# Split sums for 18 of 24 late attention pairs, and a new place for some attention pairs and plain rows

## The chip, the cores and the metric

The kernel runs on one core of a Trainium2 chip. The metric is the device time of one execution in microseconds (us). Engines are named as in the profile: PE is TensorE (PEld its weight loads), DVE is VectorE, ACT is ScalarE, POOL is GpSimd, SP is SyncE, which issues the DMAs here.

## The reference

Attention over 8 batches, 8 heads, 576 positions and a head width of 64, followed by a feed-forward layer with a softplus. All data are float32. Heads 0 to 3 attend to the last 32 positions (local), heads 4 to 7 to earlier positions of the same remainder modulo 32 (strided).

```python
def _attn_ref(q, k, v):
    scores = scale * np.matmul(q, k.transpose(0, 1, 3, 2))
    rel = pos[:, None] - pos[None, :]
    mask_local = (rel >= 0) & (rel < stride)            # stride = 32
    mask_strided = (rel >= 0) & (pos[None, :] % stride == pos[:, None] % stride)
    scores = np.where(masks[None, :, :, :], scores, -1000000000.0)
    attn = np.exp(scores - np.max(scores, axis=-1, keepdims=True))
    attn = attn / (np.sum(attn, axis=-1, keepdims=True) + 1e-09)
    return np.matmul(attn, v)
def _moe_ref(x, w_in, w_out):                           # x: 4608 x 512
    h = x @ w_in                                        # 512 x 2048
    g = np.maximum(h, 0.0) + np.log1p(np.exp(-np.abs(h)))
    return g @ w_out                                    # 2048 x 512
```

`x` is the attention's output with the heads side by side, one row per token.

## The kernel before

**Feed-forward layer.** The 4608 tokens are cut into 9 chunks of 512, numbered 0 to 8, and the 2048 features into 16 rows of 128. A row f of chunk c has two products: F c.f (`hidden`, L813) forms 128 features for 512 tokens in a PSUM bank `ph`, and O c.f (`output`, L882) multiplies them by `w_out` and adds to four accumulators `py0` to `py3`, one for each 128 tokens. Each product is made of float32 numbers split into a high and a low part, in three of the four combinations, so F or O is 12 matmuls of 512 columns, some 2.7 us. Between F and O lies the row's softplus: absolute value, exponential and logarithm on ACT (L825, L828, L830), the sum on DVE (`softplus`, L837), and the split of the outcome into `gh` (ACT, L298) and `gl` (DVE, L867). There are two `ph` banks, two `u` buffers and three `g` buffers.

When the last O of a chunk is done, `result` copies each accumulator into a buffer `o` (L298 on ACT or DVE) and SP stores it (L898). These `o` tiles come from the pool `io` with four buffers, which also serves the sums of weights (`ww`, `wh`) and the stored softplus rows that are read back (`u_in`, L852).

Chunks 0, 1 and 2 are computed row by row. Chunks 3 and 4, 5 and 6, and 7 and 8 form pairs, each computed by one level of Strassen (`pair_of_chunks`, `product`, L985) on sums of x (L1010, L1016, L1026) and sums of weights (L1032 to L1055), in banks a, b and c of which the first takes a `ph` bank. Rows 7 and 15 of the chunks with even numbers, 4 and 6, are plain rows outside the pairs (`plain`). Their other rows are stored as `u` in DRAM and come back later (`spilled`), when their O is done.

**Attention.** The 64 heads of 8 batches make 32 pairs of heads, n = 0 to 31, four to a batch. Pairs 0 to 7 are done before chunk 0; pairs 8 to 31, the late ones, each finish a piece of a later chunk's x and stand among the feed-forward rows. A late pair has two blocks on TensorE. S n is its scores (`head_scores`, L439): 36 matmul instructions in float32, each a pair of passes of 64 rows x 32 columns over 64 keys. V n is its weighted sums (`late_sums`). In the usual joint step S n is followed at once by V n-1; the sums' halves then go into the rest of S n's bank `po` and into a `ph` bank. A V that stands alone uses the banks `po` and `ps`.

Between S n and V n lies the softmax: mask and copy from PSUM (L498), maximum, subtraction, exponential on ACT (L513), row sums, reciprocal, multiplication (L542), and `turn`, which transposes blocks of 32x32 on DVE. After V n the pieces of x are cast into the tiles `x_h`, `x_l` and, for the chunk after next, `x_far` (`x_part`, ACT L730 and DVE L728).

A late pair has one of two forms. `WHOLE` says which, and before it holds all 24.

- Whole: part 1 of the scores uses the same column groups as part 0 (`place_of`, L421), so four tiles of the array are in use. `turn` is one transposition of 128x576 (L567). The sums (L600) take 32 key rows x 64 columns and up to 64 queries, 38 matmul instructions, 76 passes. `load_v` has four DMAs.
- Split: part 1 of the scores uses the other column groups, eight tiles. `turn` is one transposition of 128x576 (L571), which leaves half of the blocks in the wrong rows, and four of 32x288 (L576, L578), which set those right. The sums (L613) take 64 key rows x 64 columns over 32 queries, 36 matmul instructions, 72 passes. `load_v` has three DMAs and, where the pair before was whole, a memset on POOL (L335).

The scores of pairs 4 to 7 are in the split form's layout already.

**The order of the work.** Every step is a task for a `Plan` (L77): a name, an urgency, an engine, a cost in us and the tasks it comes after. The plan places the tasks by urgency into the engines' free spans and then writes them out by start time, which fixes each engine's order. The urgency of feed-forward steps follows a table of times `when`; `places` says behind which row each late pair stands; `far_first` is the last pair that stands ahead of the first chunk pair; the events in `pair_of_chunks` place the others. No scheduler moves anything after that.

Of the kernel before, what the change touches and what calls it, by code (L numbers as in the profile page):

```python
# [18 lines left out]
P = 128  # L19
# [57 lines left out]
class Plan:  # L77
# [8 lines left out]
    def add(self, name, urgency, engine, cost, fn, after=(), late=0.0):  # L86
        self.tasks[name] = (urgency, len(self.tasks), engine, cost, fn, after, late)
# [29 lines left out]
def attention_softplus_ffn(  # L117
# [9 lines left out]
    nc = tc.nc  # L127
    B, NPAIR, _, _, S = qk.shape
# [4 lines left out]
    NFC = DFF // P  # L133
# [10 lines left out]
    TPC = max(CH) // P  # L144
# [94 lines left out]
    taken = []  # L239
    phs, us, ghs, gls, lent = {}, {}, {}, {}, {}  # L240
    HALF = NFC // 2
    WHOLE = range(2 * NPAIR, 8 * NPAIR)
    NEAR = 3
    SPILLED = (NEAR + 1, NEAR + 3)
    PLAIN = [(c, f) for c in SPILLED for f in (HALF - 1, NFC - 1)]
# [961 lines left out]
    steps = [(c, f) for c in range(NEAR) for f in range(NFC)]  # L1207
# [1 line left out]
    steps += [(NEAR, HALF - 1), (NEAR, NFC - 1), (NEAR + 1, HALF - 1)]  # L1209
    begin = NFC + AHEAD  # L1210
    last = len(order) - 1
    far_first = 5 * NPAIR
    places = (0, 2, 5, 8, 11, 14, 16, 18, 20, 23, 25, 27, 30)
    pair_at = {begin + i: n for i, n in zip(places, range(2 * NPAIR, far_first + 1))}
    i_of = {n: i for i, n in pair_at.items()}
    alone = (last - NPAIR - 3, last - NPAIR, last)

    def joint(i):
        return pair_at.get(i, 0) > 2 * NPAIR
# [1 line left out]
    when = {}  # L1221
    t = 0.0
# [6 lines left out]
    add = plan.add  # L1229
# [18 lines left out]
    for i in range(begin, len(steps)):  # L1248
        c, f = steps[i]
        w, x = CH[c] / 384, when[i]  # L1250
# [15 lines left out]
        k = i - LAG  # L1266
        if k >= FAR0:
            continue
        c, f = steps[k]
        w = CH[c] / 384  # L1270
        x = when[i] + 2.1 * w
# [5 lines left out]
        for t in range(nt):  # L1277
# [4 lines left out]
            if f == NFC - 1:  # L1282
                e, cost, engine = (("ACT", 0.5, nc.scalar), ("DVE", 0.6, nc.vector))[t % 2]
# [15 lines left out]
    def sums_of(n):  # L1299
        late_sums(n, n not in alone)  # L1300
# [44 lines left out]
    def parts_of(n, z, made):  # L1345

        first = order[n][0] * S
        free = []
        for c in range(NCHUNK):
            if START[c] < first + S and START[c] + CH[c] > first:  # L1350
                old = [k for k in range(c) if PLACE[k] == PLACE[c]]
                if old and old[-1] >= NEAR:
                    free += [f"P{p}.{NEAR}.{HALF-2}" for p in "1256374"]
                elif old:
                    free.append(f"F{NFC * old[-1] + NFC - 1}")
                elif PLACE[c] == 3:
                    free.append(f"F{2 * NFC - 1}")
                    for g in range(12, NFC):
                        free += [f"Wt{g}", f"W1.{g-HALF}"]
        for half in range(2):  # L1360
            z += 0.6
            fn = lambda half=half: x_part(n, half, False)
            add(f"H{n}{half}", z, "ACT", 0.35, fn, [made] + free)
            fn = lambda half=half: x_part(n, half, True)
            add(f"L{n}{half}", z + 0.3, "DVE", 0.45, fn, [f"H{n}{half}"], 0.5)
        if n != last:
            add(f"v{n+1}", z + 2, "SP", 1.3, lambda: load_v(n + 1), [made], 2.0)

    for i, n in pair_at.items():
        x = when[i]  # L1370
        after, cost = needs_of(n), 1.3
        if joint(i):
            cost = 2.5
            after += [f"P{n-1}", f"v{n-1}", f"u{i-1}"]
        y = x + (12 if n == far_first else 1.5)
        scores_of(n, x, y, f"S{n}", "PE", cost, after, n - 1 if joint(i) else None)
        if n != far_first:
            parts_of(n, when[i_of[n + 1]] + 1.9, f"S{n+1}")

    SLOT = 0.234  # L1380
    now = when[len(steps)]
# [11 lines left out]
    def out_task(c, f, t, late=()):  # L1393

        name, own = f"O{c}.{f}.{t}", [f"l{g_of(c, f)}"]
        if c >= NEAR and f == ROWS[c][0]:
            free = f"y{FAR0 - 1 if c == NEAR else c - 1}.{t}"
            if c == NCHUNK - 1 and t == 0:
                free = f"j1.{c-1}.{HALF-1}"
            own.append(free)  # L1400
        on_pe(name, 3, lambda: output(c, f, (t,)), own)
        if f != ROWS[c][-1]:
            return
        if c == NCHUNK - 1 and t == TPC - 1:
            for h, (e, engine) in enumerate((("DVE", nc.vector), ("ACT", nc.scalar))):
                cols = slice(DM // 2 * h, DM // 2 * (h + 1))
                fn = lambda engine=engine, cols=cols: result(c, t, engine, cols)
                add(f"y{c}.{t}{h}", now, e, 0.35, fn, [name])
            return
        e, cost, engine = (("ACT", 0.6, nc.scalar), ("DVE", 0.7, nc.vector))[t % 2 * (c not in (NEAR, NEAR + 2))]  # L1410
        add(f"y{c}.{t}", now, e, cost, lambda: result(c, t, engine), [name, *late])

    g_users = [(NEAR - 1, NFC - 1), (NEAR, HALF - 1), (NEAR, NFC - 1)]
# [37 lines left out]
    def x_task(A, z, each, then=0.0):  # L1451

        for i in range(2):
            x_sums(A, i, z + (10 * each + then) * i, each)
# [214 lines left out]
    def plain(c, f):  # L1669

        on_pe(f"F{c}.{f}", 12, lambda: hidden(c, f), [ring[-2], *lows_of(c), *row_loads.get(f, [])])
        ring.append(f"u{c}.{f}")
        soft_task(c, f, f"F{c}.{f}")

    def spilled(A, rows, between, finish=None):

        C, end = A + 1, HALF - 2
        for g in ROWS[A][-2:]:
            for t in range(TPC):
                out_task(A, g, t)  # L1680
        if finish:
            finish()
        stored = {g: f"Us{g_of(C, g)}" for g in ROWS[C]}
        start = now
        for k, g in enumerate(ROWS[C]):
            z = start + 12 * SLOT * (k - 1)
            z += sum(slots * SLOT for at, slots, _ in between if at < k)
            if k < 2:
                after, z = [], z - 6
            elif k < 4:  # L1690
                after = [f"P1.{A}.{end}", f"P2.{A}.{end}"]
            elif k < 8:
                after = [f"u{A}.{end}", *stored.values()]
            else:
                after = [f"l{C}.{ROWS[C][k-4]}"]
            fn = lambda k=k, g=g: u_load(C, g, k - 2)
            add(f"Ul{C}.{g}", z - 5, "SP", 0.8, fn, after + [stored[g]], 2.5)
            g_task(C, g, z, f"Ul{C}.{g}", [])
        for k, g in enumerate(rows):
            for at, _, fn in between:  # L1700
                if at == k:
                    fn()
            for t in range(TPC):
                out_task(C, g, t)

    C = NEAR + 1
    for t in range(TPC):
        out_task(NEAR, HALF - 1, t)
    row_loads = {}
    plain(C, NFC - 1)  # L1710
    w_load(NEAR, 0, when[len(steps) - 1])
    x_task(NEAR, when[len(steps) - 6], 0.5, 20)
    events = {(f, "scores"): far_first + 1 + k for k, f in enumerate((1, 2, 3, 4, 5))}
    pair_of_chunks(NEAR, [(NEAR, NFC - 1, t) for t in range(TPC)], events, HALF - 1)
    n = last - NPAIR
    A = NEAR + 2
# [5 lines left out]
        (11, 12, lambda: plain(A + 1, HALF - 1)),  # L1722
        (13, 12, lambda: plain(A + 1, NFC - 1)),
        (14, 12, lambda: plain(A, HALF - 1)),
        (15, 12, lambda: plain(A, NFC - 1)),
    ]
    for f, free in (
        (HALF - 1, [f"l{C}.{g}" for g in ROWS[C][2:4]]),
# [11 lines left out]
    events = {(f, "scores"): n + 1 + k for k, f in enumerate((0, 2, 4, 6))}  # L1740
# [89 lines left out]
```

## Time and profile before

| | us |
| --- | --- |
| median of 3 runs (lowest, highest) | 869.92 (869.78, 871.36) |
| the profiled execution | 875.21 |
| its span in the trace | 873.4 |
| PE busy | 856.8 |
| DVE busy | 557.0 |
| ACT busy | 515.5 |
| L813, L882 and L985, one matmul of 512 columns | 0.39 |
| largest waits of PE behind the start: for copies `o` on DVE and on ACT | 2.0 and 1.5 |

A matmul's duration overlaps with the next one's: where nothing holds them, large matmuls start about 0.23 us apart. A row of the timeline may stand for several instructions (x4); in brackets are the idle time ahead of it and what ended it. A window's row gives the busy time and the number of instructions for each engine in that stretch, the granted clock (PEclk), the share of DMA time and the bandwidth.

### The profile page before, as it was taken

The numbers are of one execution on the slowest core, as the hardware profiler recorded it, in microseconds if no ns is written. First come the engines' busy times: TensorE is split into PE (matmuls) and PEld (weight loads), VectorE is DVE, ScalarE is ACT, GpSimd is POOL, SyncE is SP. The second block draws the span as 40 slices with busy tenths as digits, with TensorE's granted clock in tenths as the row PEclk, the third lists the DMA queues.
The fourth block names the chain that finished last, engine by engine and source line by source line (L and its number), as shares of the span: only waits on it lengthen the run. The fifth ranks groups of instructions, "written<-read, shape, count | busy, mean of one in ns | idle before, by whom it ended". The sixth has DMA issues, their size and how long they took to land.

```text
span 873.4 us, 18955 instructions
## 1 busy us (share of the span) xinstructions
PE 856.8 (98%) x7742; PEld 703.4 (81%) x7742; DVE 557.0 (64%) x1039; ACT 515.5 (59%) x958; POOL 65.8 (8%) x88
## 2 busy tenths in 40 slices
PE   7899999999999999999999999999999999999998
PEld 5787888888888887788888887888888888888886
DVE  7699987777677787456665773445567545656500
ACT  6798746555565574667677444677675355556400
POOL 6245550000000000000000000000000000000000
PEclk9899999999999999999999999999999999999999
DMA  9694215754533643655663734455455144334000
GB/s 319 213 393 139 74 60 162 242 191 163 193 103 105 186 139 108 205 175 174 190 189 135 218 101 157 139 198 179 143 173 185 61 134 135 117 123 132 37 36 25
DMA packets 96119, 134.23 MB, mean 154 GB/s; under 512 B 37664, under 2 KB 57760, under 8 KB 96032
## 3 DMA queue, kind: packets, MB, share of 16 engines
q1 hardware_dynamic: 95744, 132.69, 46.9%
q8 instruction: 61, 1.00, 0.5%
q10 hardware_dynamic: 288, 0.33, 0.1%
q14 instruction: 26, 0.21, 0.1%
HBM read 98.39 MB, written 34.60 MB: 152 GB/s over the span
## 4 chain that ended last, share of the span: by engine, by line
PE 91%; DVE 4%; ACT 2%; issue 2%; DMA 1%; POOL 0%; SPq 0%; ACTq 0%; DVEq 0%; POOLq 0%
PE py L882 42%; PE ph L813 14%; PE bank_a L985 14%; PE bank_c L985 7%; PE bank_b L985 3%; PE pv L600 3%; PE ps L439 2%; PE py_last L882 1%; PE po L439 1%; PE pv L679 1%; PE pt L649 1%; PE po L600 1%; DVE home L553 1%; DVE a_i L767 0%; DMA raw_q<-in_qk_dram 0%
## 5 line engine op out<-in xcount | busy, mean ns | idle before, releaser
L882 PE MATMUL py<-w_o,gh 128*128 128x512 f32 x1024 | 318.4, 392 | 3.5 <-DVE o L298 2.0
L882 PEld LDWEIGHTS py<-w_o,gh 128*128 128x128 f32 x1024 | 190.4, 188 | 45.0 <-DVE o L298 3.4
L882 PE MATMUL py<-w_o,gl 128*128 128x512 f32 x512 | 199.5, 390 | 0.1
L813 PE MATMUL ph<-x_h,w_i 128*128 128x512 f32 x416 | 129.4, 392 | 1.8 <-DVE x_far L728 1.3
L882 PEld LDWEIGHTS py<-w_o,gl 128*128 128x128 f32 x512 | 96.1, 188 | 20.7 <-issue 0.5
L298 ACT CAST gh<-u 128x512 fp32r<-128x512 f32 x101 | 62.7, 622 | 76.8 <-DVE u L837 36.8
L867 DVE TENSOR_TENSOR gl<-u,gh 128x512 fp32r<-128x512 f32 x115 | 79.0, 688 | 28.2 <-ACT gh L298 25.6
L813 PEld LDWEIGHTS ph<-x_h,w_i 128*128 128x128 f32 x416 | 77.3, 188 | 19.6 <-issue 1.3
L828 ACT ACTIVATE u<-u 128x512 f32<-128x512 f32 x144 | 91.1, 633 | 3.2
L830 ACT ACTIVATE u<-u 128x512 f32<-128x512 f32 x144 | 90.4, 631 | 3.4
L813 PE MATMUL ph<-x_l,w_i 128*128 128x512 f32 x208 | 81.0, 389 | 0.0
L825 ACT ACTIVATE u<-ph 128x512 f32<-128x512 f32 x56 | 33.3, 597 | 57.5 <-PE ph L813 54.9
L825 ACT ACTIVATE u<-kept 128x512 f32<-128x512 f32 x66 | 41.7, 631 | 39.8 <-DVE kept L1085 29.9
L837 DVE SCALAR_TENSOR_TENSOR u<-ph,u 128x512 f32<-128x512 f32 x56 | 38.3, 683 | 26.5 <-ACT u L830 26.4
L1085 DVE TENSOR_TENSOR kept<-bank_c,kept 128x512 f32<-128x512 f32 x22 | 15.2, 692 | 50.6 <-PE bank_c L985 49.2
L813 PEld LDWEIGHTS ph<-x_l,w_i 128*128 128x128 f32 x208 | 39.1, 188 | 8.4
L298 DVE COPY o<-py 128x512 f32<-128x512 f32 (+1 forms) x13 | 8.7, 668 | 52.3 <-PE py L882 48.1
L1080 ACT COPY kept<-bank_a 128x512 f32<-128x512 f32 x44 | 25.8, 587 | 26.4 <-PE bank_a L985 26.4
L1085 DVE TENSOR_TENSOR kept<-bank_b,kept 128x512 f32<-128x512 f32 x22 | 15.2, 692 | 36.9 <-PE bank_b L985 36.9
L298 ACT COPY home<-home 128x576 f32<-128x576 f32 x26 | 33.2, 1276 | 6.4 <-DMA home<-in_qk_dram 6.3
L298 ACT COPY o<-py 128x512 f32<-128x512 f32 (+1 forms) x23 | 12.8, 575 | 40.9 <-PE py L882 27.5
L985 PE MATMUL bank_a<-t,away 128*128 128x512 f32 x132 | 33.8, 391 | 0.2
(199 smaller groups left out, 1463.8 us busy)
## 6 DMA issues: line engine op xcount, KB each, us to landing
ws<-far SPq DMA_DIRECT2D x44, 512.0 KB, 3.7
home<-in_qk_dram SPq DMA_DIRECT2D x56, 288.0 KB, 3.4
near<-far_w SPq DMA_DIRECT2D x23, 512.0 KB, 3.3
out_dram<-o SPq DMA_DIRECT2D x35, 256.0 KB, 2.4
ri<-in_moe_w_in_dram SPq DMA_DIRECT2D x16, 512.0 KB, 8.0
ro<-in_moe_w_out_dram SPq DMA_DIRECT2D x16, 512.0 KB, 8.6
far_w<-w_i SPq DMA_DIRECT2D x16, 512.0 KB, 4.0
far_u<-kept SPq DMA_DIRECT2D x28, 256.0 KB, 2.7
```

The source lines that it names most:

```text
L298: (engine.copy if engine is nc.scalar else engine.tensor_copy)(dst, src)
L439: nc.tensor.matmul(pss[n, part][to : to + 32, at : at + 64], lhsT=qT[head, c : c + 32], rhs=k_of(n)[head, c : c + 64], start=True, stop=True,)
L600: nc.tensor.matmul(to[place][64 * h : 64 * h + 64, at : at + hi - lo], lhsT=v_whole[rows, x], rhs=turned_all[rows, lo:hi], start=x + place ...
L813: nc.tensor.matmul(ph, lhsT=w_i(c, f)[:, half, cc * P : (cc + 1) * P], rhs=x_at(x, cc, c), start=(i == 0), stop=(i == 3 * NCC - 1),)
L825: nc.scalar.activation(us[c, f], phs[c, f], AF.Abs)
L828: nc.scalar.activation(u, u, AF.Exp, scale=-1.0)
L830: nc.scalar.activation(u, u, AF.Ln, bias=1.0)
L837: nc.vector.scalar_tensor_tensor(to, in0=ph, scalar=0.0, in1=u, op0=ALU.max, op1=ALU.add)
L867: engine.tensor_tensor(g, us.pop((c, f)), ghs[c, f].bitcast(F32), op=ALU.subtract)
L882: nc.tensor.matmul(y_of(c, t), lhsT=g[:, sl], rhs=w32["o", f][:, half], start=(f == ROWS[c][0] and n == 0), stop=(f == ROWS[c][-1] and n = ...
L985: nc.tensor.matmul(bank, lhsT=w_left(p, A, f, half, i), rhs=x_right(p, A, part, i), start=p in "125" and n == 0, stop=n == 5, skip_group_c ...
L1085: nc.vector.tensor_tensor(t, bank_of(p, A, f), t, op=ALU.add)
```

## The change

`WHOLE` shrinks from 24 pairs to six, 13 and 16 to 20. The other 18 take the split form. Pair 19 is now the last ahead of the first chunk pair, with its sums alone; the scores of pair 20 move behind row 0 of chunks 3 and 4. The casts of x after joint sums get an urgency 1.2 us earlier. The result copies of chunks 3 and 5 alternate between ACT and DVE as the others do. The plain row F4.15 is planned ahead of O3.7, and the plain row F5.15 one product later, behind O4.14.

```diff
-    WHOLE = range(2 * NPAIR, 8 * NPAIR)
+    WHOLE = (13, 16, 17, 18, 19, 20)
...
-    far_first = 5 * NPAIR
-    places = (0, 2, 5, 8, 11, 14, 16, 18, 20, 23, 25, 27, 30)
+    far_first = 5 * NPAIR - 1
+    places = (0, 2, 5, 8, 11, 14, 16, 18, 20, 22, 24, 26)
...
-    alone = (last - NPAIR - 3, last - NPAIR, last)
+    alone = (far_first, last - NPAIR - 3, last - NPAIR, last)
...
-        y = x + (12 if n == far_first else 1.5)
+        y = x + 1.5
         scores_of(n, x, y, f"S{n}", "PE", cost, after, n - 1 if joint(i) else None)
-        if n != far_first:
-            parts_of(n, when[i_of[n + 1]] + 1.9, f"S{n+1}")
+        if n == far_first:
+            made, z = f"V{n}", when[i + 3] + 0.6
+            add(made, when[i + 3], "PE", 1.3, lambda n=n: sums_of(n), [f"P{n}", f"v{n}"])
+            parts_of(n, z, made)
+        else:
+            parts_of(n, when[i_of[n + 1]] + 0.7, f"S{n+1}")
...
-        e, cost, engine = (("ACT", 0.6, nc.scalar), ("DVE", 0.7, nc.vector))[t % 2 * (c not in (NEAR, NEAR + 2))]
+        e, cost, engine = (("ACT", 0.6, nc.scalar), ("DVE", 0.7, nc.vector))[t % 2]
...
-        for k, g in enumerate(rows):
+        for k in range(len(rows) + 1):
             for at, _, fn in between:
                 if at == k:
                     fn()
-            for t in range(TPC):
-                out_task(C, g, t)
+            for t in range(TPC if k < len(rows) else 0):
+                out_task(C, rows[k], t)
...
+    row_loads = {}
+    plain(C, NFC - 1)
     for t in range(TPC):
         out_task(NEAR, HALF - 1, t)
-    row_loads = {}
-    plain(C, NFC - 1)
     w_load(NEAR, 0, when[len(steps) - 1])
-    x_task(NEAR, when[len(steps) - 6], 0.5, 20)
-    events = {(f, "scores"): far_first + 1 + k for k, f in enumerate((1, 2, 3, 4, 5))}
+    x_task(NEAR, when[len(steps) - 5], 0.5, 10)
+    events = {(f, "scores"): far_first + 1 + k for k, f in enumerate((0, 1, 2, 3, 4, 5))}
...
-        (15, 12, lambda: plain(A, NFC - 1)),
+        (16, 12, lambda: plain(A, NFC - 1)),
```

Behind the attention and ahead of the first chunk pair TensorE runs, in blocks, before: F2.15, O2.12, F3.7, S20, V19, F3.15, F4.7, O2.13, O2.14, O2.15 mixed with O3.7, F4.15. After: O2.12, F2.15, V19, F3.7, O2.13, F3.15, F4.7, F4.15, O2.14, O2.15, O3.7. Here is the end of that on TensorE, before, where `gh_2_15` marks O2.15 and `gh_3_7` marks O3.7:

```order
L882 MATMUL py0_106<-w_o_15_1759,gh_2_15_4234 128x512 x2
L882 MATMUL py0_106<-w_o_15_1759,gl_2_15_4318 128x512
L882 MATMUL py0_106<-w_o_7_1277,gh_3_7_4405 128x512 x2
L882 MATMUL py0_106<-w_o_7_1277,gl_3_7_4419 128x512
L882 MATMUL py1_107<-w_o_15_1759,gh_2_15_4234 128x512 x2
L882 MATMUL py1_107<-w_o_15_1759,gl_2_15_4318 128x512
L882 MATMUL py2_108<-w_o_15_1759,gh_2_15_4234 128x512 x2
L882 MATMUL py2_108<-w_o_15_1759,gl_2_15_4318 128x512
L882 MATMUL py1_107<-w_o_7_1277,gh_3_7_4405 128x512 x2
```

The same place after:

```order
L882 MATMUL py0_106<-w_o_15_1759,gh_2_15_4332 128x512 x2
L882 MATMUL py0_106<-w_o_15_1759,gl_2_15_4339 128x512
L882 MATMUL py1_107<-w_o_15_1759,gh_2_15_4332 128x512 x2
L882 MATMUL py1_107<-w_o_15_1759,gl_2_15_4339 128x512
L882 MATMUL py2_108<-w_o_15_1759,gh_2_15_4332 128x512 x2
L882 MATMUL py2_108<-w_o_15_1759,gl_2_15_4339 128x512
L882 MATMUL py3_109<-w_o_15_1759,gh_2_15_4332 128x512 x2
L882 MATMUL py3_109<-w_o_15_1759,gl_2_15_4339 128x512
L882 MATMUL py0_106<-w_o_7_1277,gh_3_7_4337 128x512 x2
```

Before, O3.7 begins anew in an accumulator directly behind that accumulator's last products of chunk 2; after, all of O2.15 stands in between, and F4.15, which stood behind O3.7, now stands ahead of O2.14.

On TensorE at the change from chunk 4 to chunks 5 and 6, before, where the first row is the end of F5.15, `gh_4_14` marks O4.14 and `gh_5_7` marks O5.7:

```order
L813 MATMUL ph_5_15_6446<-x_far_3_4326,away_5_5718 128x512 x3
L882 MATMUL py0_106<-w_o_14_1464,gh_4_14_6362 128x512 x2
L882 MATMUL py0_106<-w_o_14_1464,gl_4_14_6397 128x512
L882 MATMUL py1_107<-w_o_14_1464,gh_4_14_6362 128x512 x2
L882 MATMUL py1_107<-w_o_14_1464,gl_4_14_6397 128x512
L882 MATMUL py2_108<-w_o_14_1464,gh_4_14_6362 128x512 x2
L882 MATMUL py2_108<-w_o_14_1464,gl_4_14_6397 128x512
L882 MATMUL py3_109<-w_o_14_1464,gh_4_14_6362 128x512 x2
L882 MATMUL py3_109<-w_o_14_1464,gl_4_14_6397 128x512
L882 MATMUL py0_106<-w_o_7_1277,gh_5_7_6459 128x512 x2
```

The same place after:

```order
L882 MATMUL py3_109<-w_o_14_1464,gh_4_14_6386 128x512 x2
L882 MATMUL py3_109<-w_o_14_1464,gl_4_14_6441 128x512
L813 MATMUL ph_5_15_6488<-x_far_0_3713,away_5_5735 128x512 x3
L813 MATMUL ph_5_15_6488<-x_far_2_3893,away_5_5735 128x512 x3
L813 MATMUL ph_5_15_6488<-x_far_1_4089,away_5_5735 128x512 x3
L813 MATMUL ph_5_15_6488<-x_far_3_4281,away_5_5735 128x512 x3
L882 MATMUL py0_106<-w_o_7_1277,gh_5_7_6472 128x512 x2
```

F5.15 moved from ahead of O4.14 to behind it. With it moved the load of the stored row `u_in_6_15` on SP, from between the first and the second store of chunk 4's results to behind all four.

On DVE, pair 8's turn and what stands behind it (`home_1` is the pair's buffer, `u_1_3` and `gl_1_3` belong to the softplus of F1.3, `ww` to the sums of weights), before:

```order
L542 TENSOR_TENSOR home_1_95<-home_1_95,st_8_1891 128x576
L567 STREAM_TRANSPOSE home_1_95<-home_1_95 128x576
L837 SCALAR_TENSOR_TENSOR u_1_3_1946<-ph_1_3_1911,u_1_3_1946 128x512
L1055 TENSOR_TENSOR ww_0_4_1840<-ww_0_4_1840,wh_0_4_1929 128x512
L867 TENSOR_TENSOR gl_1_3_1975<-u_1_3_1946,gh_1_3_1973 128x512
```

The same place after:

```order
L542 TENSOR_TENSOR home_1_95<-home_1_95,st_8_1891 128x576
L571 STREAM_TRANSPOSE home_1_95<-home_1_95 128x576
L837 SCALAR_TENSOR_TENSOR u_1_3_1946<-ph_1_3_1911,u_1_3_1946 128x512
L576 STREAM_TRANSPOSE home_1_95<-home_1_95 32x288 x2
L867 TENSOR_TENSOR gl_1_3_1975<-u_1_3_1946,gh_1_3_1973 128x512
L578 STREAM_TRANSPOSE home_1_95<-home_1_95 32x288 x2
L1055 TENSOR_TENSOR ww_0_4_1840<-ww_0_4_1840,wh_0_4_1929 128x512
```

The four pieces stand between rows of the softplus, and the sums of weights moved behind them.

## The prediction

> **What bounds the kernel now.** I read the page first, then the chain that ended last, then the windows and the timeline of TensorE around the attention blocks, and last the rows just ahead of TensorE's few waits. The page's busy line and the chain by engine:
>
> ```profile
> PE 856.8 (98%) x7742; PEld 703.4 (81%) x7742; DVE 557.0 (64%) x1039; ACT 515.5 (59%) x958; POOL 65.8 (8%) x88
> PE 91%; DVE 4%; ACT 2%; issue 2%; DMA 1%; POOL 0%; SPq 0%; ACTq 0%; DVEq 0%; POOLq 0%
> ```
>
> TensorE is busy for 98% of the span and carries 91% of the chain. So two things can shorten the run: TensorE's own work, and the few places at which it waits. A microsecond on another engine costs nothing until TensorE waits for it.
>
> The profiled execution took 875.21 us and the median of the runs is 869.92 us, 5.3 us less. I make the sum on the profiled execution and carry its difference over to the median unchanged.
>
> **TensorE's own work: the scores.** The change gives 18 of the 24 late pairs the split form. Its scores are already in the trace, since pairs 4 to 7 use them: the same 36 instructions in this pair of windows, but part 1 goes to the other two column groups, so that eight tiles are in use and not four. The windows of one late pair's scores, of pair 4's scores, of pair 9's scores with pair 8's sums behind them, and of one late pair's sums, each from its first matmul to the next large one:
>
> ```profile
> 138.21:139.35 1.14, 1.14 (x74) 1.05 (x73) 0.18 (x1) 0.00 (x0) 0.00 (x0) 1.00 1.04 370
> 36.93:37.92 0.99, 0.99 (x73) 0.90 (x73) 0.99 (x2) 0.96 (x2) 0.47 (x1) 1.00 1.10 395
> 150.47:152.89 2.42, 2.42 (x149) 2.29 (x148) 1.96 (x4) 2.02 (x4) 0.00 (x0) 1.00 0.91 288
> 254.96:256.24 1.28, 1.28 (x83) 1.24 (x77) 0.56 (x1) 0.85 (x2) 0.00 (x0) 1.00 0.30 33
> ```
>
> 1.14 against 0.99 us is 0.148 us a pair before rounding. 18 pairs x 0.148 = **2.7 us less**.
>
> **TensorE's own work: the sums.** A whole pair's sums take 1.28 us (fourth window): 76 passes of 32 rows x 64 columns with up to 64 moving queries, four at a time. Each round of four takes 58.5 ns, since 13 rounds lie between the first two rows here (19 rounds make 1.11 us, which leaves a tail of 0.17 us); the other two rows are the end of another pair's sums, where passes over 32 queries only follow each other:
>
> ```profile
> 255.18 0.22 PE L600 MATMUL pv<-home,home 32*64 32x64 f32 x2
> ...
> 255.94 0.22 PE L600 MATMUL pv<-home,home 32*64 32x64 f32 x2
> ...
> 228.50 0.26 PE L600 MATMUL po<-home,home 32*64 32x32 f32 x4
> 228.54 0.31 PE L600 MATMUL pv<-home,home 32*64 32x64 f32 x6
> ```
>
> The split form does 72 passes of 64 rows x 64 columns over 32 queries, in 18 rounds of four. No such block is in the trace, so I bound it. If a round is set by the columns that move, it takes about half of 58.5 ns, 30 ns, near the 40 ns or less between the last two rows; 18 rounds and the tail make 0.71 us. If a round is set by something that does not shrink with them, it stays at 58.5 ns and the block takes 18 x 0.0585 + 0.17 = 1.22 us. Between them: pair 4's scores reach 72 passes in 0.99 - 0.17 = 0.82 us, 11.4 ns a pass, which would be 46 ns a round and 0.99 us. The nearest row in kind is that of the 32-query passes, but it covers four passes only, so I take 0.85 us, 38 ns a round. That is 0.43 us less a pair, 18 x 0.43 = **7.8 us less**, with ends of 10.3 and 1.1 us.
>
> What speaks for the halved round are the weight loads: the loads of 64 columns and of 32 columns in the groups by line:
>
> ```profile
> L600 PEld LDWEIGHTS pv<-home,home 32*64 32x64 f32 x1068 | 30.2, 133 | 3.3 <-PE py L882 0.7 <-issue 0.7
> L439 PEld LDWEIGHTS ps<-home,home 64*32 64x32 f32 x1344 | 23.9, 106 | 9.9 <-issue 8.5 <-ACT u L825 0.7 <-ACT u L830 0.4
> ```
>
> A load of 64 columns takes 27 ns more than one of 32, yet in the late scores, with 32 columns, four-tile rounds take 1.14 - 0.17 = 0.97 us over 18 rounds, 54 ns, hardly less than 58.5. So the loads have not set the round so far; whether they set it when the moving columns are halved, no row tells. The Trainium skill's page "TensorE: Matmul & The Clock Gate", section "LDWEIGHTS (loading the stationary operand)", says that a load takes its number of columns divided by 1.2 ns, whatever the rows. The difference of 27 ns is just what it gives for 32 columns; by that rule a load of 64 columns would take an estimated 53 ns, and if loads of four tiles shared one path the round could not go below that. The block would then take an estimated 1.12 us, and 2.9 us would stand in the place of the sum's 7.8 us; this is rival A's case.
>
> **TensorE's waits that the new order takes away.** Three places. First F3.15 behind the sums of pair 19 (TensorE, then DVE):
>
> ```profile
> 332.70 0.31 PE L600 MATMUL pv<-home,home 32*64 32x64 f32 x6
> 334.28 0.70 PE L813 MATMUL ph<-x_h,w_i 128*128 128x512 f32 x2 [1.26 <-DVE x_far L728]
> ...
> 333.82 0.31 DVE L728 TENSOR_TENSOR x_far<-pv,x_far 128x160 fp32r<-128x160 f32 x1
> ```
>
> Joint sums put their second half into a bank of the two that `hidden` uses. F3.15 needs that bank and starts 0.15 us after DVE has emptied it. In the usual rhythm (228.54 to the next block took 0.24 us) it would have started at 332.94: 1.34 us lost. In the new order pair 19's sums stand alone and use the scores' and sums' own banks, with F3.7 behind them, so this wait goes.
>
> Second, O3.7 runs through the four accumulators of chunk 2 as ACT and DVE empty them; the large matmuls here start 0.23 us apart when nothing holds them:
>
> ```profile
> 345.73 0.39 PE L882 MATMUL py<-w_o,gl 128*128 128x512 f32 x1
> 346.79 0.73 PE L882 MATMUL py<-w_o,gh 128*128 128x512 f32 x2 [0.68 <-ACT o L298]
> ...
> 351.19 0.39 PE L882 MATMUL py<-w_o,gl 128*128 128x512 f32 x1
> 352.36 0.74 PE L882 MATMUL py<-w_o,gh 128*128 128x512 f32 x2 [0.79 <-DVE o L298]
> ```
>
> 1.06 - 0.23 = 0.83 and 1.17 - 0.23 = 0.94 us. In the new order all of O2.15 (2.7 us) stands ahead of O3.7's first quarter, and an accumulator has three quarters of a product, about 2.0 us, to be emptied in; a copy takes 0.6 to 0.7 us. Nothing is left of this wait if the copies come at once.
>
> Third, O5.7 after O4.14 in the same way, with the two copies that held it:
>
> ```profile
> 539.84 0.39 PE L882 MATMUL py<-w_o,gl 128*128 128x512 f32 x1
> 541.00 0.73 PE L882 MATMUL py<-w_o,gh 128*128 128x512 f32 x2 [0.78 <-ACT o L298]
> 541.57 0.40 PE L882 MATMUL py<-w_o,gl 128*128 128x512 f32 x1
> 543.16 0.73 PE L882 MATMUL py<-w_o,gh 128*128 128x512 f32 x2 [1.19 <-DVE o L298]
> ...
> 540.36 0.58 ACT L298 COPY o<-py 128x512 f32<-128x512 f32 x1 [2.38 <-DMA out_dram<-o]
> ...
> 542.41 0.69 DVE L298 COPY o<-py 128x512 f32<-128x512 f32 x1 [4.18 <-DMA out_dram<-o]
> ```
>
> 0.93 + 1.36 = 2.29 us. The copies waited for a buffer that an earlier result was being stored from, since a load of a stored softplus row holds the fourth. In the new order that load comes after the four copies, and F5.15 (2.72 us) stands between O4.14 and O5.7. Together 1.34 + 1.77 + 2.29 = **5.4 us less**.
>
> **What the change adds.** Taking the sums of pair 19 and the scores of pair 20 out of one joint block adds one transition, 1.14 + 1.28 against 2.42 us, which rounds to nothing; I enter 0.1 us for the rounding.
>
> The split form needs more turning on DVE. One whole turn and the nearest row for its four added pieces of 32x288:
>
> ```profile
> L567 DVE STREAM_TRANSPOSE home<-home 128x576 f32<-128x576 f32 x24 | 18.7, 777 | 3.5 <-PE pv L600 3.0
> ...
> L553 DVE STREAM_TRANSPOSE home<-home 32x192 f32<-32x192 f32 x32 | 11.6, 363 | 0.3
> ```
>
> By a straight line between 192 columns in 0.363 and 576 in 0.777 us, 288 columns take 0.47 us, and 0.40 from start to start, since rows on DVE overlap by some 0.07. That is 4 x 0.40 = 1.6 us a pair, 29 us over 18 pairs, on an engine that is busy for 557 of 873 us. It costs only where TensorE waits. In the Strassen stage a pair stands like this (three rows of DVE, then the first of its sums on TensorE):
>
> ```profile
> 397.80 0.77 DVE L567 STREAM_TRANSPOSE home<-home 128x576 f32<-128x576 f32 x1
> ...
> 401.95 0.69 DVE L837 SCALAR_TENSOR_TENSOR u<-bank_a,u 128x512 f32<-128x512 f32 x1 [2.08 <-ACT u L830]
> ...
> 402.38 0.24 PE L600 MATMUL pv<-home,home 32*64 32x32 f32 x2
> ```
>
> The turn ends 3.8 us ahead of the sums and DVE idles for 2.08 us between: the 1.6 us go into that hole, at no cost. Without the hole they would cost 1.6 us in each pair. Pair 8 has no such hole:
>
> ```profile
> 148.72 0.78 DVE L567 STREAM_TRANSPOSE home<-home 128x576 f32<-128x576 f32 x1
> 149.42 0.65 DVE L837 SCALAR_TENSOR_TENSOR u<-ph,u 128x512 f32<-128x512 f32 x1
> 150.00 0.67 DVE L1055 TENSOR_TENSOR ww<-ww,wh 128x512 fp32r<-128x512 f32 x1
> ...
> 151.61 0.24 PE L600 MATMUL pv<-home,home 32*64 32x32 f32 x2
> ```
>
> The new order on DVE is turn, softplus of F1.3 (0.58 to the next start), two pieces, the low half of its g (0.6), two pieces. From 149.42 that is 150.00, 150.80, 151.41, and the end near 152.2. The sums would want to start at 151.61 less the 0.3 us that two scores blocks save, 151.3; with a hand-over of 0.15 us they start about **0.9 us late** (between 0.5 and 1.6). Queued behind on TensorE is the next product, O of chunk 1, which loses the same.
>
> F3.15, F4.7 and F4.15 now stand back to back on two banks. F4.15 needs the bank of F3.15, and there is only F4.7, 2.72 us, to run that row's softplus:
>
> ```profile
> L837 DVE SCALAR_TENSOR_TENSOR u<-ph,u 128x512 f32<-128x512 f32 x56 | 38.3, 683 | 26.5 <-ACT u L830 26.4
> ...
> L825 ACT ACTIVATE u<-ph 128x512 f32<-128x512 f32 x56 | 33.3, 597 | 57.5 <-PE ph L813 54.9
> ...
> L828 ACT ACTIVATE u<-u 128x512 f32<-128x512 f32 x144 | 91.1, 633 | 3.2
> ```
>
> 0.60 + 2 x 0.63 + 0.68 = 2.54 us (the logarithm as long as the exponential), plus three hand-overs of 0.15 us (as at 334.28): 3.0, **0.3 us late**. The first product of chunks 3 and 4 needs F4.7's bank, whose softplus now stands behind chunk 2's copies on ACT and DVE (0.6 and 0.7 us); against the cover of O2.14, O2.15 and O3.7 I enter 0.4 us, between 0 and 1.4. The result copies of chunks 3 and 5 go half to DVE and the casts of x move earlier: covered by the Strassen rows around them, nothing.
>
> **Sum.** -2.7 - 7.8 - 5.4 + 0.1 + 0.9 + 0.3 + 0.4 = -14.2 us: 875.2 becomes 861.0 in a profiled execution like this one, and 869.9 becomes **855.7 us** as a median.
>
> **The rivals.**
> A, weight loads set the round: it stays at the 54 to 58.5 ns of the four-tile rounds in the trace, and the sums save 0.06 to 0.14 us a pair, 1.8 us in the middle over 18. Then -14.2 + 6.0 = -8.2: 861.7 us. For it: loads last 133 ns each and are busy for 81% of the span. Against: the 32-query passes at 228.50, and scores rounds that did not get shorter with shorter loads.
> B, the turns come late everywhere, and the kernel gets slower: DVE's added 1.6 us end behind the time at which the sums are due, in most of the 18 pairs. Place: between the last piece of a turn and the first split sum. The gain without pair 8's wait is 15.1 us, so it decides from 15.1 / 18 = 0.84 us a pair, and to be measured as slower from 0.94. With the full 1.6 us it gives 869.9 - 15.1 + 28.8 = 883.6 us. For it: pair 8, and softplus rows that are put between the pieces. Against: the 3.8 us of the Strassen stage, and an idle third of DVE.
> C, the result waits come back: a copy still stands behind other work, now on DVE between casts and sums of x, and O3.7 and O5.7 wait as before, or F4.15 and the first product wait for 2 to 3 us. Either gives back about 5 us: 861 us. For it: half of the copies of chunks 3 and 5 now share DVE with softplus rows. Against: 2 to 2.7 us of TensorE work stand in between now.
>
> **How the numbers follow.** 0.62 for the forecast, 0.17 for A, 0.12 for C, 0.05 for B, and 0.04 for small gains and losses that cancel. The range: the sums at 0.70 us and no added wait give -2.7 - 10.3 - 5.4 = -18.4, 851.5 us; A with its sums at 1.22 us and the added waits doubled gives -2.7 - 1.1 - 5.4 + 3.4 = -5.8, 864.1 us. So 851 to 864.5. A measurement of this kernel can tell about 0.2%, 1.7 us, from no change. Faster by more takes the forecast, A and C: 0.91. Within: 0.04. Slower: B, 0.05.
>
> **What would show it.** Of the profile of the changed kernel: a split pair's scores block at 0.99 us; its sums, from the first L613 matmul to the next block, at 0.85 us (0.70 to 0.99; 1.1 or more is A). No wait over 0.3 us on TensorE ahead of F3.15, O3.7 and O5.7. A wait of about 0.9 us ahead of pair 8's sums, for a DVE turn, and none for a turn in the Strassen stage. The forecast is wrong if waits for a turn stand ahead of many sums (B), or if TensorE's busy time falls by less than 6 us (A).

## The result and the profile after

| | before | after |
| --- | --- | --- |
| median of the runs (lowest to highest), us | 870.64 (869.78 to 871.79) | 859.44 (858.68 to 861.16) |
| the profiled execution, us | 875.21 | 858.68 |
| its span, us | 873.4 | 856.9 |
| PE busy, us | 856.8 | 848.0 |
| DVE busy, us | 557.0 | 593.6 |

The change makes the kernel 11.2 us faster in the median, a ratio of 0.9873 with a 95% interval of 0.9853 to 0.9894. The forecast was 14.2 us less.

The busy line and the chain by engine of the changed kernel:

```profile
PE 848.0 (99%) x7670; PEld 696.9 (81%) x7670; DVE 593.6 (69%) x1115; ACT 512.4 (60%) x954; POOL 66.9 (8%) x91
PE 90%; DVE 3%; DMA 3%; ACT 2%; issue 1%; POOL 0%; SPq 0%; ACTq 0%; DVEq 0%; POOLq 0%
```

TensorE still sets the time. The two profiled executions differ by 16.5 us, 5.3 more than the medians, and that surplus lies in the start, ahead of anything that the change touches. Two windows of before, then the same two of after:

```profile
20.00:24.20 4.20, 0.38 (x13) 0.24 (x9) 1.60 (x3) 0.49 (x2) 3.16 (x3) 0.86 0.79 281
24.20:28.00 3.80, 3.79 (x60) 3.79 (x60) 1.22 (x3) 1.95 (x5) 0.61 (x1) 0.50 0.05 17
```

```profile
20.00:24.20 4.20, 3.66 (x110) 3.52 (x107) 3.27 (x7) 3.32 (x10) 3.30 (x3) 1.00 0.75 274
24.20:28.00 3.80, 3.72 (x58) 3.12 (x53) 3.37 (x7) 3.43 (x9) 0.87 (x2) 1.00 0.49 150
```

In the profile of before TensorE stands still for almost 4 us here, and the clock that is granted to it afterwards is 0.50. In the profile of after it works through. The length of this wait differs from one profiled execution to the next (0.3 to 3.8 us in the traces of this study), so I compare the traces from pair 4's scores on, at 36.93 us before and 31.31 after. From there to the last matmul the changed kernel takes 10.8 us less, close to the medians' 11.2.

The windows that answer to those of before: a split pair's scores, its predecessor's split sums, a whole pair's scores, a whole pair's sums:

```profile
163.73:164.72 0.99, 0.99 (x73) 0.90 (x72) 0.90 (x3) 0.77 (x2) 0.00 (x0) 1.00 0.15 58
164.72:165.90 1.18, 1.18 (x78) 1.14 (x72) 1.18 (x3) 0.37 (x1) 0.00 (x0) 1.00 0.90 333
260.27:261.41 1.14, 1.14 (x73) 1.05 (x72) 1.01 (x3) 1.00 (x2) 0.00 (x0) 1.00 0.15 57
274.88:276.16 1.28, 1.28 (x82) 1.24 (x76) 0.56 (x1) 0.86 (x2) 0.00 (x0) 1.00 0.04 13
```

The scores do what was forecast, 0.99 us instead of 1.14. The sums do not: 1.18 us against 1.28, where 0.85 was forecast. Two rows of these sums, 13 rounds apart:

```profile
164.86 0.23 PE L613 MATMUL po<-home,home 64*64 64x32 f32 x2
...
165.62 0.23 PE L613 MATMUL po<-home,home 64*64 64x32 f32 x2
```

0.76 us over 13 rounds is 58.5 ns a round, to the tenth what it was with twice the moving columns.

The waits of TensorE in the changed kernel, by line and releaser:

```profile
PE ph L813 <- DVE u L837: 0.4, 1, 0.4
...
PE py L882 <- ACT o L298: 0.2, 1, 0.2
...
PE pv L613 <- DVE home L578: 0.2, 1, 0.2
```

The first line stands at 74 us and was 0.5 us before. The waits for copies `o` (2.0 and 1.5 us in this view before) have shrunk to one of 0.2 us behind pair 13's sums, and the one for `x_far` is gone. F3.15, O3.7 and O5.7 do not wait. The last line is pair 8:

```profile
145.23 0.51 PE L613 MATMUL po<-home,home 64*64 64x32 f32 x3
...
146.00 0.24 PE L613 MATMUL pv<-home,home 64*64 64x32 f32 x1 [0.20 <-DVE home L578]
...
147.16 0.50 PE L882 MATMUL py<-w_o,gh 128*128 128x512 f32 x1
```

This block takes 147.16 - 145.23 = 1.93 us, 0.75 more than its 1.18. The view shows 0.20 us of it as a wait; the rest hides in the duration of the few matmuls that started in between, since ends of matmuls are modelled. Starts are safer to read than idle times.

Nowhere else does a turn stop the sums for over 0.2 us, but the room has become small. Pair 21's turn on DVE:

```profile
386.55 0.77 DVE L571 STREAM_TRANSPOSE home<-home 128x576 f32<-128x576 f32 x1
387.32 0.69 DVE L867 TENSOR_TENSOR gl<-u,gh 128x512 fp32r<-128x512 f32 x1
388.04 0.97 DVE L576 STREAM_TRANSPOSE home<-home 32x288 f32<-32x288 f32 x2
389.03 0.97 DVE L578 STREAM_TRANSPOSE home<-home 32x288 f32<-32x288 f32 x2
```

Two pieces take 0.97 us, 0.49 from start to start, not 0.40. The turn ends at 390.00 and the sums begin at 390.99: 0.99 us ahead, where it was 3.8 us for the same pair.

### The profile page after: what moved, and what is told of

It reads as the page before. It is cut to its first block, busy times and chain, and to the rows that moved or that the text cites. A ratio compares the mean times of both kernels' runs of the same rounds, so it can differ in the third digit from the quotient of the medians.

```text
span 856.9 us, 18842 instructions
## 1 busy us (share of the span) xinstructions
PE 848.0 (99%) x7670; PEld 696.9 (81%) x7670; DVE 593.6 (69%) x1115; ACT 512.4 (60%) x954; POOL 66.9 (8%) x91
## 4 chain that ended last, share of the span: by engine, by line
PE 90%; DVE 3%; DMA 3%; ACT 2%; issue 1%; POOL 0%; SPq 0%; ACTq 0%; DVEq 0%; POOLq 0%
PE py L882 42%; PE ph L813 14%; PE bank_a L985 14%; PE bank_c L985 7%; PE bank_b L985 3%; DMA ro<-in_moe_w_out_dram 2%; PE ps L439 2%; PE po L613 2%; PE py_last L882 1%; PE pv L613 1%; PE po L439 1%; PE pv L679 1%; PE pv L600 1%; PE pt L649 1%; DVE home L553 1%
## 5 line engine op out<-in xcount | busy, mean ns | idle before, releaser
L828 ACT ACTIVATE u<-u 128x512 f32<-128x512 f32 x144 | 91.1, 634 | 3.2
L298 DVE COPY o<-py 128x512 f32<-128x512 f32 (+1 forms) x17 | 11.4, 674 | 48.2 <-PE py L882 46.4
L298 ACT COPY o<-py 128x512 f32<-128x512 f32 (+1 forms) x19 | 10.7, 573 | 39.0 <-PE py L882 27.9
```

Source lines behind the costliest of these rows:

```text
L298: (engine.copy if engine is nc.scalar else engine.tensor_copy)(dst, src)
L828: nc.scalar.activation(u, u, AF.Exp, scale=-1.0)
```

## The experiments

Each kernel ran beside the kernel before on the same chip. Where one is compared with the changed kernel, the difference is that of the two ratios times 871 us.

**The form alone.** All in the old order.

```diff
-    WHOLE = range(2 * NPAIR, 8 * NPAIR)
+    WHOLE = (13, 16, 17, 18, 19, 20)
```

> The kernel before with the new set of whole pairs and nothing else, so 18 pairs are split in the old order. Theory (the loads of 64 columns set the round): scores 0.99 us instead of 1.14 in 18 pairs, sums 1.18 instead of 1.28, one wait of some 0.75 us for a turn at pair 8: 2.7 + 1.8 - 0.75, about 3.7 us less than before. Rival (the form is worth more and the new order spends it on waits for turns): 6 us or more less, with no wait for a turn.

Measured: medians of 865.86 and 871.18 us; the ratio over all runs, 0.9946 (0.9932 to 0.9959), makes 4.7 us less, with the interval from 3.6 to 5.9. From pair 4's scores on its trace is 4.65 us shorter than that of before. Scores and sums measured as in the changed kernel, and pair 8 waits in the same way. The old waits are all there:

```profile
PE py L882 <- DVE o L298: 2.1, 2, 1.3
...
PE py L882 <- ACT o L298: 1.6, 2, 0.9
PE ph L813 <- DVE x_far L728: 1.3, 1, 1.3
```

So the form is worth 4 to 5 us. That is 1 us above the theory's 3.7, which the interval still holds, and under the rival, whose condition (no wait for a turn) is not met. Of the trace's surplus, 0.7 us are two short stretches inside the sums of pairs 15 and 25 in the profile of before, 0.5 and 0.2 us; whether they belong to the whole form is open.

**The order alone.** The changed kernel with every late pair whole.

```diff
-    WHOLE = (13, 16, 17, 18, 19, 20)
+    WHOLE = range(2 * NPAIR, 8 * NPAIR)
```

> The changed kernel with all 24 late pairs whole, so the new places without the new form. Theory (the two parts add): 11.2 - 3.7, about 7.5 us less than before, of which 5.7 us are the waits ahead of F3.15, O3.7 and O5.7; sums 1.28 us, scores 1.14 us. Rival (the waits that went were short because the split form had shifted the engines): about 4 us less or under, with waits of some 1 us left ahead of O3.7 or O5.7.

Measured: 865.15 against 871.18, ratio 0.9931 (0.9918 to 0.9943), 6.0 us less, with the interval from 5.0 to 7.1. That is less than the theory's 7.5 and more than the rival's 4. No wait for a copy or for `x_far` is left, so the rival's condition is not met; its profile shows two short waits that the changed kernel's does not have (0.7 us at a Strassen product, 0.4 us for a load of `v`), which I take for chance. 0.9946 x 0.9931 = 0.9877, and the changed kernel has 0.9873: the two halves add, and the order is somewhat the larger.

**Twice the moving columns.** Every split sum streams 64 queries.

```diff
+                    y = x - x % 2 if x < NCHK - 1 else x - 1
...
-                        to[place][64 * h : 64 * h + 64, 32 * x : 32 * x + 32],
+                        to[place][64 * h : 64 * h + 64, 32 * y : 32 * y + 64],
...
-                        rhs=turned[rows, place_of(x // 6, h), x],
+                        rhs=turned[rows, place_of(x // 6, h), y : y + 2],
```

> The changed kernel, but every split sum streams 64 queries where it needs 32 (it adds nothing right: the outputs of neighbouring spans overwrite each other). Theory (the load of 64 columns sets the round, the columns that move lie beside it): the round stays at 58.5 ns and the block at 1.18 us. Rival (a tile's load and its matmul follow each other, some 28 ns and 30 ns): the round grows to about 86 ns, the block to about 1.70 us.

This kernel and the next one ran once (859.75 and 860.34 us); what counts is the block in the trace. The block of pair 9's sums, and two rows 13 rounds apart:

```profile
165.37:166.58 1.21, 1.21 (x78) 1.14 (x73) 1.21 (x3) 0.29 (x1) 0.00 (x0) 1.00 0.93 340
```

```profile
165.48 0.22 PE L614 MATMUL po<-home,home 64*64 64x64 f32 x2
...
166.24 0.23 PE L614 MATMUL po<-home,home 64*64 64x64 f32 x2
```

The round is 58.5 ns again. The 0.03 us more come at the block's first round. Load and matmul of a tile do not follow each other, then, and with 64 loaded columns the number of moving ones, 32 or 64, is of no account.

**Half the loaded columns.** Where a split pair's sums stand alone, each pass loads 32 columns.

```diff
+        wide = D if joint else 32
...
-                        to[place][64 * h : 64 * h + 64, 32 * x : 32 * x + 32],
-                        lhsT=v_late[rows, x, D * h : D * h + D],
+                        to[place][64 * h : 64 * h + wide, 32 * x : 32 * x + 32],
+                        lhsT=v_late[rows, x, D * h : D * h + wide],
```

> The changed kernel, but the sums of the pairs whose sums stand alone and are split (24, 27 and 31) load 32 columns where they need 64, so half of the features are left out; one wide pass of 288 queries per half and head stands ahead. Theory (the load sets the round): the rounds of these blocks fall from 58.5 to some 30 ns. Rival 1 (load and matmul follow each other): some 44 ns. Rival 2 (every pass costs some 14.6 ns to issue, whatever its size): 58.5 ns as before.

The 72 narrow passes of pair 24 (one row of the timeline holds them all), from their first start to the next large matmul:

```profile
465.44 0.85 PE L623 MATMUL pv<-home,home 64*32 64x32 f32 x72
466.22 0.50 PE L892 MATMUL py<-w_o,gh 128*128 128x512 f32 x1
```

0.78 us instead of 1.18. The last of the 72 starts 0.66 us after the first, which is 9.2 ns a pass and 37 ns a round in the mean; by the starts of the single passes the rounds of the first half are 31.8 ns apart and those at the end 33, with an uneven stretch between. So what set 58.5 ns was neither the issue of a pass nor its moving columns, but the load of 64 columns. A pass that loads half the columns also writes half as many rows of its bank, which these runs do not separate; the load is the nearer reading, since the rounds differ by 26.7 ns and a load of 64 columns lasted 27 ns more than one of 32 in the profile of before. The Trainium skill's page "TensorE: Matmul & The Clock Gate", section "LDWEIGHTS (loading the stationary operand)", gives columns divided by 1.2 ns, an estimated 53 ns for 64 columns and 27 ns for 32. That is one load; a round of four tiles took 5 ns more than that in both cases, so the loads of four tiles do not add up here.

**Pair 8 whole as well.**

```diff
-    WHOLE = (13, 16, 17, 18, 19, 20)
+    WHOLE = (8, 13, 16, 17, 18, 19, 20)
```

> The changed kernel with pair 8 whole too. Theory (pair 8's split form buys 0.15 + 0.10 us and pays 0.75 us for its late turn): the wait ahead of its sums goes and the kernel takes some 0.5 us less than the changed one, about 11.7 us less than before. Rival (the wait moves to the next block on TensorE, O of chunk 1, which waits for the same DVE rows): no less than the changed kernel.

Measured: 858.86 us, ratio 0.9865 (0.9850 to 0.9879). In its trace no sum waits for a turn, and from pair 4's scores on it is 0.52 us shorter than the changed kernel's. The trace says what the theory said, but 0.5 us is less than the runs can tell: the intervals of the two kernels overlap. It has the lowest ratio of this study.

**No whole pair left.**

```diff
-    WHOLE = (13, 16, 17, 18, 19, 20)
+    WHOLE = ()
```

> The changed kernel with no whole pair left, so 13 and 16 to 20 are split too. Theory (a split turn ends some 2.8 us later than a whole one, and these six whole turns stand 2.3 to 9.2 us ahead of their sums): only pair 20 gets a wait of some 0.5 us, and 6 x 0.25 us are saved, so some 1 us less than the changed kernel. Rival (ahead of the first chunk pair DVE has no room for 6 x 1.6 us, and casts, sums of x and softplus rows come late): waits of TensorE of over 2 us in all between pairs 13 and 20, and 1 us or more above the changed kernel.

Measured: ratio 0.9893 (0.9877 to 0.9910), 1.7 us above the changed kernel; the two intervals overlap, but its trace shows the loss, 1.5 us from pair 4's scores on. The rival was right, though not at the turns themselves. Its waits in the stretch ahead of the first chunk pair:

```profile
289.48 0.25 PE L613 MATMUL pv<-home,home 64*64 64x32 f32 x2 [0.64 <-DVE u L837]
...
345.23 0.73 PE L882 MATMUL py<-w_o,gh 128*128 128x512 f32 x2 [1.35 <-DVE o L298]
346.42 0.73 PE L985 MATMUL bank_a<-x_h,near 128*128 128x512 f32 x2 [0.23 <-DVE u L837]
```

DVE is busy for 11 us more (604.4 against 593.6), most of it in a stretch in which DVE is already busy for 84.4 of 103 us in the changed kernel (240 to 343 us) and for 91.1 of 105 us here (240 to 345), and what comes late is a softplus row and a copy of chunk 2's results. So by the traces the choice of six whole pairs is worth some 1.5 us.

**F5.15 back ahead of O4.14.**

```diff
-        (16, 12, lambda: plain(A, NFC - 1)),
+        (15, 12, lambda: plain(A, NFC - 1)),
```

> The changed kernel with one line undone: F5.15 is planned where it was, ahead of O4.14. Theory: the load of the stored row takes the fourth buffer again, two copies of chunk 4's results wait for stores, and O5.7 waits for some 2.3 us in all; 2.3 us more than the changed kernel. Rival (the waits went because of other moves of the change): the same time as the changed kernel.

Measured: ratio 0.9903 (0.9889 to 0.9918), 2.6 us above the changed kernel, with intervals that overlap a little. Both waits of O5.7 are back, in size and cause:

```profile
530.39 0.74 PE L882 MATMUL py<-w_o,gh 128*128 128x512 f32 x2 [0.86 <-ACT o L298]
532.66 0.73 PE L882 MATMUL py<-w_o,gh 128*128 128x512 f32 x2 [1.29 <-DVE o L298]
```

By starts they lose 1.0 + 1.5 = 2.5 us. A single row's place, which decides whether a load takes the fourth buffer of a pool, is almost half of what the new order brings.

**The last two pieces of each split turn three times.**

```diff
-                nc.vector.transpose(turned[lower, 1], src[upper, 0])
+                for _ in range(3):
+                    nc.vector.transpose(turned[lower, 1], src[upper, 0])
```

> The changed kernel, but the last two pieces of each split turn are done three times over, 4 x 0.40 = 1.6 us more on DVE a pair. Theory (TensorE pays only what lies beyond the time by which a turn is ahead, 0.98 us at pairs 21 to 23, 0.8 at 26, 1.5 at 27, nothing at 8, over 2.6 elsewhere): 3 x 0.65 + 0.8 + 0.1 + 1.6, about 4.5 us more than the changed kernel, with waits at those five pairs alone or with 14. Rival 1 (DVE is never late): no more than 0.5 us more. Rival 2 (DVE's time counts in full): 18 x 1.6 = 29 us more.

Measured: 873.42 us, ratio 1.0025 (1.0015 to 1.0035), 13 us above the changed kernel. I expected 4.5. It is neither rival: the 18 pairs add 35 us to DVE. Where TensorE waited:

```profile
PE pv L614 <- DVE home L579: 5.1, 6, 1.2
PE ps L439 <- DVE x_l L729: 2.0, 1, 2.0
...
PE po L614 <- DVE home L579: 1.2, 1, 1.2
...
PE bank_b L986 <- DVE home L498: 0.6, 1, 0.6
```

Sums waited for a turn at pairs 8, 21, 22, 23, 26 and 27, just those that the theory lists. But the added pieces are 4 x 0.49 = 1.9 us and not 1.6, the DVE rows behind them come late in turn (casts `x_l`, the mask at L498, a softplus row at pair 15), and TensorE's clock falls behind the two waits at pair 8:

```profile
145.00:150.00 5.00, 2.56 (x74) 2.33 (x72) 4.80 (x10) 0.97 (x3) 0.00 (x0) 0.78 0.11 39
150.00:154.40 4.40, 4.40 (x12) 3.47 (x11) 4.14 (x10) 1.95 (x5) 0.00 (x0) 0.50 0.93 271
```

At a clock of 0.50 the large matmuls start 0.43 us apart instead of 0.23, which costs some 2 us, and the rounds of pair 8's sums ahead of them 0.105 us apart instead of 0.0585, some 0.8 us more. My theory counted the first wait of each pair and left out what stands behind it.

**The copies of chunks 3 and 5 back on ACT.**

```diff
-        e, cost, engine = (("ACT", 0.6, nc.scalar), ("DVE", 0.7, nc.vector))[t % 2]
+        e, cost, engine = (("ACT", 0.6, nc.scalar), ("DVE", 0.7, nc.vector))[t % 2 * (c not in (NEAR, NEAR + 2))]
```

> The changed kernel with the result copies of chunks 3 and 5 on ACT alone, as before the change. Theory (these copies lie beside Strassen rows and nobody on TensorE waits for them): the same time as the changed kernel within 0.7 us. Rival (they are a part of the gain): 1 us or more above the changed kernel, with waits of TensorE ahead of rows 0 and 1 of chunks 3 and 5.

Measured: ratio 0.9888 (0.9873 to 0.9902), 1.3 us above the changed kernel, with intervals that overlap by more than half. No row 0 or 1 of chunks 3 or 5 waits in its trace, so the rival's mechanism isn't there; its trace is 1.3 us longer by short waits at pairs 25 and 26 (by starts 0.4 us for a load of `v` and 0.6 us for a turn) and less. That is more than the theory's 0.7 us; whether the copies have a part in these waits, or chance alone, stays open.

**The casts of x 1.2 us later.**

```diff
-            parts_of(n, when[i_of[n + 1]] + 0.7, f"S{n+1}")
+            parts_of(n, when[i_of[n + 1]] + 1.9, f"S{n+1}")
```

> The changed kernel with the urgency of the casts of x after joint sums put back by 1.2 us, as before the change. Theory (the casts feed the next joint step's banks, which comes 10 us or more later, so 1.2 us are covered): the same time as the changed kernel within 0.7 us. Rival (without the earlier casts the split turns push them behind and the next scores or product wait): 1 us or more above the changed kernel, with waits of TensorE for x_l or x_h.

Measured: ratio 0.9902 (0.9885 to 0.9918), 2.5 us above the changed kernel; the intervals just overlap. Its trace has a wait for a cast and a new one for a softplus row, neither of which the changed kernel has:

```profile
PE ph L813 <- DVE u L837: 1.7, 2, 1.3
...
PE ph L813 <- DVE x_l L728: 0.4, 1, 0.4
```

By the trace the theory fell: this number, which I had entered at nothing, keeps some 1.7 us of waits away (1.25 us for the softplus row, 0.4 us for the cast). The runs alone, with intervals that overlap, would not show it. The numbers of a plan cannot be costed one by one, since moving one urgency moves other rows on DVE with it. Another 1.2 us in that profile is a wait for a load of `v`, which the other traces have at 0.4 us or not at all; I take that for chance. With the slower clock behind it (last section) it makes the profiled execution, 864.80 us, the longest of the four; the others took 860.21 to 862.13.

## Why the prediction was right, and where it was off

The sign and the range were right, and so were the scores, the waits and pair 8's turn. The largest term, the sums, was not. Term by term, from the starts of rows in the two traces:

| term of the sum | forecast | measured |
| --- | --- | --- |
| scores of 18 pairs | -2.7 | -2.7 |
| sums of 18 pairs | -7.8 | -1.8 |
| waits ahead of F3.15, O3.7, O5.7 | -5.4 | -5.7 |
| pair 8's turn | +0.9 | +0.75 |
| F4.15, the first product, the split joint block | +0.8 | +0.6 |

The sums are 18 x 0.10 = 1.8 us. The waits come to 5.7 us because the three places held a further one of 0.27 us in O3.7 that I did not count. In the last line, F4.15 lost 0.2 us ahead of its first matmul and 0.1 behind it, the two blocks made of the joint one 0.2 us and the first product 0.1.

**The step that failed is "The nearest row in kind is that of the 32-query passes, but it covers four passes only, so I take 0.85 us, 38 ns a round".** The round is 58.5 ns. I argued that loads had not set the round so far, since 32 and 64 loaded columns gave 54 and 58.5 ns. But in both of these 64 columns moved. With the two experiments all four cases of a four-tile round are measured; the first is the whole pairs' scores of before, where eight rounds lie between these two rows of its timeline, 56 ns a round:

```profile
138.68 0.29 PE L439 MATMUL po<-home,home 64*32 64x64 f32 x8
...
139.13 0.29 PE L439 MATMUL po<-home,home 64*32 64x64 f32 x8
```

| ns a round | 32 columns move | 64 columns move |
| --- | --- | --- |
| 32 columns loaded | 31.8 | 56 |
| 64 columns loaded | 58.5 | 58.5 |

The four cases fit a round that takes the longer of load and movement. Before, both had 64 columns and were level, so halving the movement alone could bring nothing. Why the four passes at the end of a whole pair's sums came closer together was not tried; that no loads follow them would fit.

That is rival A, to which I gave 0.17, at its price for the sums (1.1 to 2.5 us). Its total of 861.7 us is 2.3 us above the measured time; the forecast of 855.7 is 3.7 us below it. Of my two signs for A, the length of the block gave the right answer (1.18 us, where 1.1 or more was to be A). The other, that TensorE's busy time falls by less than 6 us, was badly set: it fell by 8.8 us. Of these, 2.7 us lie ahead of pair 4's scores, where the profile of before ran at half the clock for a while, and the 6.1 us that are left still miss the sign.

The measured terms make -8.9 us and the traces differ by 10.8. The other 2 us lie in rows that no term covers. In the profile of before these are 0.5 and 0.2 us inside the sums of pairs 15 and 25, 0.4 us in the row behind pair 13's sums, 0.3 us at a row at 319.42, 0.6 us behind the six waits in the table (the second matmul behind a wait starts 0.30 to 0.34 us after the first and not 0.23), and 0.45 us between the scores of pairs 4 and 8, where TensorE's rows are the same in both kernels. The other way, the changed kernel has 0.3 us behind pair 13's sums and 0.1 us each in pair 21's sums and ahead of pair 26's scores. Why these places differ was not sought.

So the total came nearer than its parts deserve. The sums alone were 6.0 us short, and the traces only 3.4 us short of 14.2, because of these 2 us and of small errors that went the other way. That was luck, and the range held the result since it had been drawn out to A's end.

Rival B, the turns late everywhere, did not come, but its condition is nearer than I said. I read 3.8 us of room in the Strassen stage and charged 1.6 us; the turn took 2.0 us more and ended 2.8 us later, since the plan put other DVE rows between its pieces. The tripled turn shows the other side of the edge: 1.9 us more a pair and the whole gain is gone. Rival C came in no form; that F5.15's place alone brings O5.7's waits back shows that it was a real one.

## What to carry to other kernels

Before halving one operand of a small matmul, find out which of load, movement and issue sets the rounds: a round that stays the same when one of them is changed says only that another is at least as long. Read a rate from steady rounds, never from the last passes of a block. And charge a longer step off the critical path with what the scheduler will put between its pieces, against the room left at the tightest place and not at a typical one.

## What the runs showed of the hardware

- A wait of TensorE can cost more than its length. From the end of the second of two waits of 1.2 us at pair 8 in the tripled run the granted clock was 0.50 for 6.8 us: 2.2 us of the first window shown there, all 4.4 us of the second and the rest behind it. In the run with late casts it was 0.50 for 3.4 us behind a single wait of 1.2 us (two windows of that run; the second begins 0.1 us ahead of the slower clock):

```profile
474.80:477.40 2.60, 1.40 (x74) 1.27 (x72) 1.18 (x3) 0.73 (x1) 0.00 (x0) 1.00 0.80 263
477.40:480.90 3.50, 3.50 (x12) 2.72 (x9) 3.24 (x8) 2.96 (x8) 0.00 (x0) 0.52 1.09 342
```

  Waits of 1.3 and 1.2 us in the profile of before (334.28 and 543.16) were followed by matmuls 0.23 us apart, full speed. The Trainium skill's page "TensorE: Matmul & The Clock Gate", section "Part 1: The HAM clock gate", says that activity is judged in windows of some 3.4 us that run freely, and puts half the clock behind at least one idle window. The lengths of 3.4 and 6.8 us agree with one and two such windows, and that a wait of one length sometimes costs a window and sometimes not agrees with their running freely. That a wait of 1.2 us, a third of a window, is enough does not agree with an idle window; here the traces decide.
- Short transpositions on DVE, 32x288, did not overlap: 0.49 us from start to start, and 0.97 for two, where I had read an overlap of 0.07 us from other rows.
- Eight tiles did not double the rate of four. Of the 72 passes of split scores the first stand alone on four tiles; in the other 48, in which both parts alternate over eight, a pass starts every 11.1 ns in the mean, unevenly, against 14.0 ns for the whole form's four tiles with the same 32 loaded and 64 moving columns. Why was not tried.
